# Column 0 centred only and scaled after its products; coarser weight loads; row gathers issued after the last transposes

## Chip, cores, metric

One core of one Trainium2 chip. The metric is the device time of one execution in microseconds (us). A profile's span is some 1.8 us shorter than this time. The kernel before takes 179.18 us (median of 3 runs, 179.08 to 179.73).

## The reference

```python
xn = layernorm(x)                                   # x: 2048 x 512, bf16; mean and variance by row
A  = irfft2(rfft2(xn) * (w_r + 1j * w_i))           # spectral filter
B  = (gelu(xn @ w_gate) * (xn @ w_up)) @ w_down     # 512 -> 1792 -> 512
return x + A + B
```

## The kernel before

The rows of x are kept as 16 columns of 128 rows. TensorE does both halves: the products with w_gate and w_up (`g_ps`, `u_ps`, in 14 blocks of 128 features), and the transform as products with tables (VectorE folds `A` and `xf`, then `bp`, a copy `Bs`, then `dp`, and so on). A small list scheduler written in Python orders all operations from estimated durations when the program is built. The kernel then issues them in this order on each engine. At run time semaphores alone decide when something starts, so the scheduler's durations and dependencies change the order only.

```python
    load_x(0, 1); d_ident = load_ct("ident", "ident", "ACT"); load_x(1, 1)
    load_w(0, 2, ("SP", "ACT"))     # blocks 0-1 of both weights, 256 KB each
    ...
    load_x(2, 2); load_w(2, 4); load_w(4, 6); load_x(4, 4); load_w(6, 10); load_x(8, 4); load_w(10, 14)
    ...
    def layernorm(c0, n, due, after=(), halves=1):
        ...                         # statistics, ve = var + eps (VectorE), then rstd on GpSimd:
        r = add("POOL", 0.55, lambda: nc.gpsimd.tensor_tensor(out=rstd[:, k], in0=ve[:, k], in1=half[:, k], op=ALU.pow), ...)
        ...                         # xn = (x - mean) * rstd on VectorE, in 'halves' pieces
    ...
    FIRST = [(0, 1, 0, 4), (1, 1, 0, 4), (0, 2, 4, 2), (2, 2, 0, 2), (2, 2, 2, 2), (2, 2, 4, 2)]  # column, columns, block, blocks
    for c, n, f, nf in FIRST + [(0, 4, f, 1) for f in range(6, NFC)]:
        glu(c, n, f, nf)
    ...
    def fold(cg, t):                # four columns: two operations into A, two into xf (VectorE)
        ...
        a2 = dve(0.61, f2, (a0, a1), t, new=(xb,), use=(ab,))
        a3 = dve(0.61, f3, (a2,), t, use=(ab, xb))
        for q in range(4):          # bp: the first product needs a2 only, the second needs a3
            ...
            p = pe(0.222, mm, (a2, a3, d_rf), t + 1, new=(sb,), use=(xb,))
            PS_[cg, q] = act(0.53, ev, (p,), t - 5, use=(sb,))    # ScalarE copies bp into Bs
    ...
    # rows of the filter table TW, fetched by index on GpSimd
    d_tw.append(dma(P * n * 2, lambda ...: gather(k, s, c, a, n), [g_idx] + XN[11], 20, eng="POOL", issue=1.2))
```

## Time and profile before

| | kernel before |
|---|---|
| median, 3 runs | 179.18 us |
| span of the profiled run | 177.6 us |
| TensorE busy | 98% |
| first gate matmul | 6.89 us |
| last matmul starts | 174.70 us |

The timelines: start, busy us, engine, line, operation, out<-in.

```profile
40.96 0.68 DVE L567 TENSOR_TENSOR xf<-A 128x1024 bf16<-128x1024 bf16 x1
41.89 1.06 PE L581 MATMUL bp<-RF_t,xf 128*128 128x128 bf16 x16
...
44.69 0.68 DVE L567 TENSOR_TENSOR xf<-A 128x1024 bf16<-128x1024 bf16 x1
46.24 1.06 PE L581 MATMUL bp<-RF_t,xf 128*128 128x128 bf16 x16
```

VectorE is not the bound: 40.90 of 49 us. But its third fold ends at 41.64, and the third bp starts at 41.89. The bp's second product, 0.22 us later, is the first that needs the end of the fold. So the slack there is 0.47 us (1.09 us at the fourth), in a queue that is otherwise full.

### The profile page before, as it was taken

The page shows a single profiled execution, that of the slowest core. Times are in us where ns is not written, and L with a number is a line of the kernel's source. Part 1 is how long each engine was busy: PE and PEld are TensorE (multiplying, and loading weights), DVE is VectorE, ACT ScalarE, POOL GpSimd, SP SyncE. Part 2 cuts the span into 40 slices and gives each one's busy share as a digit, 9 for nine tenths or more (in the row PEclk, how much of TensorE's full clock was granted, in tenths as well). Part 3 has the DMA queues.
Part 4 walks back from the last instruction along what each step waited for, and adds up shares of the span by engine and source line. Part 5 has one row for each costly group of instructions (what it writes and reads, how often), then busy time and mean ns, then how long its engine had stood idle before and what let it go on. Part 6 is the DMA issues. An engine that isn't in the chain of part 4 may idle for free.

```text
span 177.6 us, 3041 instructions
## 1 busy us (share of the span) xinstructions
PE 173.4 (98%) x1100; PEld 92.9 (52%) x1100; DVE 118.1 (66%) x266; ACT 87.4 (49%) x158; POOL 18.6 (10%) x33
## 2 busy tenths in 40 slices
PE   6999999999999999999999999999999999999993
PEld 2598545545554544554555455554445444544463
DVE  1869999999537995889999885336442541632522
ACT  3162437456789737999998855453111211211100
POOL 3212138743200000000000000000000000000000
PEclk9999999999999999999999999999999999999999
DMA  5999487999297001302211121100222221322212
GB/s 144 311 355 359 86 270 84 223 296 193 52 347 255 2 0 29 93 2 59 61 48 37 37 59 37 27 0 0 84 68 66 83 89 59 92 80 69 74 45 59
DMA packets 23182, 19.24 MB, mean 108 GB/s; under 512 B 8512, under 2 KB 21824, under 8 KB 23168
## 3 DMA queue, kind: packets, MB, share of 16 engines
q1 hardware_dynamic: 22176, 17.57, 35.0%
q0 software_dynamic: 320, 1.19, 3.1%
q10 hardware_dynamic: 672, 0.30, 0.6%
q8 instruction: 8, 0.13, 0.3%
q14 instruction: 6, 0.05, 0.1%
HBM read 13.28 MB, written 2.10 MB: 87 GB/s over the span
## 4 chain that ended last, share of the span: by engine, by line
PE 91%; ACT 3%; DVE 3%; issue 1%; POOL 0%; DVEq 0%; POOLq 0%
PE u_ps L502 25%; PE g_ps L502 25%; PE warm L380 3%; ACT E L652 2%; PE yp L818 2%; PE bp L581 2%; PE gp L767 2%; PE yp__2078 L872 2%; PE yp__1994 L872 2%; PE yp__1967 L872 2%; PE yp__1936 L872 2%; PE yp__1909 L872 2%; PE yp__1820 L872 2%; PE yp__1793 L872 2%; PE yp__1762 L872 2%; PE yp__1735 L872 2%
## 5 line engine op out<-in xcount | busy, mean ns | idle before, releaser
L502 PE MATMUL g_ps<-xnT,Wg_sb 128*128 128x512 bf16 (+2 forms) x264 | 58.1, 347 | 0.0
L502 PE MATMUL u_ps<-xnT,Wu_sb 128*128 128x512 bf16 (+2 forms) x264 | 57.9, 347 | 0.0
L527 DVE TENSOR_TENSOR hT<-u_ps,ge 128x512 bf16<-128x512 f32 x56 | 38.4, 685 | 17.5 <-PE u_ps L502 14.4
L519 ACT ACTIVATE ge<-g_ps 128x512 bf16<-128x512 f32 x56 | 33.5, 598 | 30.5 <-PE g_ps L502 26.5
L502 PEld LDWEIGHTS <-Wu_sb 128*128 128x128 bf16 x264 | 24.3, 98 | 22.3 <-DMA Wu_sb<-in_B_w_up_dram 0.2
L502 PEld LDWEIGHTS <-Wg_sb 128*128 128x128 bf16 x264 | 24.3, 98 | 20.7 <-issue 0.2
L872 PEld LDWEIGHTS <-hT 128*128 128x128 bf16 x252 | 23.0, 98 | 21.9
L824 ACT CAST yf<-yp 128x512 bf16<-128x512 f32 x16 | 9.3, 586 | 37.6 <-PE yp L818 37.6
L652 ACT CAST E<-ep 64x512 bf16<-64x512 f32 x32 | 18.5, 579 | 1.1 <-PE ep L646 0.7
L396 DVE BATCH_NORM_STATS2 st<-x_t 128x6 f32<-128x512 bf16 x16 | 10.5, 676 | 4.8 <-DMA x_t<-in_A_x_dram 4.8
L629 ACT CAST ds<-dp 128x512 bf16<-128x512 f32 x16 | 8.8, 589 | 1.1 <-PE dp L624 1.0
L773 ACT CAST Gs<-gp 128x512 bf16<-128x512 f32 x16 | 8.6, 593 | 1.0 <-PE gp L767 1.0
L406 POOL TENSOR_TENSOR rstd<-ve,half 128x2 f32<-128x2 f32 (+2 forms) x7 | 6.6, 949 | 21.9 <-DVE ve L404 21.9
L585 ACT CAST Bs<-bp 128x512 bf16<-128x512 f32 x16 | 8.3, 603 | 0.5 <-PE bp L581 0.5
L818 PEld LDWEIGHTS <-Gs 128*128 128x128 bf16 x64 | 4.8, 98 | 3.5
L380 PE MATMUL warm<-warm 128*128 128x512 bf16 (+1 forms) x14 | 5.1, 539 | 1.3 <-POOL half L373 1.3
L412 DVE TENSOR_SCALAR xn<-x_t,mv,rstd 128x512 bf16<-128x512 bf16 (+1 forms) x17 | 6.1, 399 | 0.3 <-POOL rstd L406 0.3
L818 PE MATMUL yp<-CT,Gs 128*128 128x128 bf16 x64 | 6.0, 219 | 0.0
L683 DVE TENSOR_TENSOR m<-X,TW 128x1024 bf16<-128x1024 bf16 x8 | 5.5, 692 | 0.2
L624 PEld LDWEIGHTS <-Bs 128*128 128x128 bf16 x64 | 4.4, 98 | 2.4
L689 DVE TENSOR_TENSOR m<-X,TW 128x1024 bf16<-128x1024 bf16 x8 | 5.5, 684 | 0.0
L646 PE MATMUL ep<-ds,CT 128*128 128x512 bf16 x16 | 5.4, 379 | 0.0
(103 smaller groups left out, 169.0 us busy)
## 6 DMA issues: line engine op xcount, KB each, us to landing
y<-in_A_x_dram SPq DMA_DIRECT2D x16, 128.0 KB, 2.1
F<-F SPq DMA_DIRECT2D x32, 64.0 KB, 2.0
out_dram<-y SPq DMA_DIRECT2D x15, 128.0 KB, 1.7
Wd_sb<-in_B_w_down_dram SPq DMA_DIRECT2D x2, 896.0 KB, 8.3
x_t<-in_A_x_dram SPq DMA_DIRECT2D x3, 512.0 KB, 6.8
Wg_sb<-in_B_w_gate_dram SPq DMA_DIRECT2D x2, 512.0 KB, 6.8
Wu_sb<-in_B_w_up_dram SPq DMA_DIRECT2D x2, 512.0 KB, 9.1
Wg_sb<-in_B_w_gate_dram SPq DMA_DIRECT2D x3, 256.0 KB, 5.1
```

The lines of the kernel that those rows point to most:

```text
L380: nc.tensor.matmul(tiles["warm"][:, 0:w], lhsT=warm[:, 0:P], rhs=warm[:, 0:w], start=True, stop=True)
L396: V.bn_stats(out=st[:], in_=x_t[:, c])
L502: nc.tensor.matmul(tiles[f"{nm}.{key}"][:, f * w:f * w + w], lhsT=W[:, e, (f0 + f) * P:(f0 + f + 1) * P], rhs=rhs(e), start=(f + e == 0), ...
L519: nc.scalar.activation(out=e[:, 0:nf * w], in_=tiles[f"g_ps.{key}"][:, 0:nf * w], func=AF.Gelu_apprx_tanh)
L527: V.tensor_tensor(out=out, in0=tiles[f"u_ps.{key}"][:, 0:nf * w].rearrange("p (f w) -> p f w", w=w) if nf > 1 else tiles[f"u_ps.{key}"][:, ...
L585: nc.scalar.copy(out=o, in_=tiles[f"bp.{cg}.{q}"][:].rearrange("p c (r g a) -> p (c r) g a", r=2, a=4))
L629: nc.scalar.copy(out=ds[:].rearrange("p (s k t) -> p s k t", s=2, t=2), in_=tiles[f"dp.{G}"][:].rearrange("p s t k -> p s k t"))
L652: nc.scalar.copy(out=tiles[f"E.{g}"][64 * h:64 * h + 64, r], in_=tiles[f"ep.{g}.{h}"][64 * r:64 * r + 64])
L773: nc.scalar.copy(out=o, in_=tiles[f"gp.{g}.{h}"][:].rearrange("p q (n a) -> p (q n) a", a=4))
L818: nc.tensor.matmul(yp[:, q], lhsT=tiles["G"][:, q, c], rhs=IQ[q], start=(q == 0), stop=(q == 3), skip_group_check=True)
L824: nc.scalar.copy(out=tiles[f"yf.{c // 2}"][:, c % 2], in_=tiles[f"yp.{c}"][:])
L872: nc.tensor.matmul(y[:, s], lhsT=tiles[sb, f][:, cl * P:(cl + 1) * P], rhs=Wd_sb[:, f, s], start=(f == 0), stop=False)
```

## The change

Intent: get TensorE to useful work earlier. Column 0 is only centred, and goes to TensorE without waiting for rstd on GpSimd. Its two PSUM tiles are scaled afterwards with 1/std, which one FP32 matmul of ones with a diagonal spreads over the partitions. The weights of the first blocks come in coarser pieces, the order of the first blocks changes, and ScalarE takes over the statistics of column 3. The planner's dependency of the gathers moves to the transposes of columns 12 to 15.

```diff
-    load_w(0, 2, ("SP", "ACT"))
+    d_g = [load_first(e, eng) for e, eng in ((0, "ACT"), (2, "SP"))]      # Wg blocks 0-3, two halves of 256 KB
+    d_u = load(..., Wu_sb[:, :, 0:4 * P] ..., land=7.0)                   # Wu blocks 0-3, 512 KB
-    load_w(2, 4)
-    load_w(4, 6)
+    load_w(4, 8, (9.2, 10.6))                                             # Wg, Wu blocks 4-7, 512 KB each
     load_x(4, 4, 12.4)
-    load_w(6, 10)
+    load_w(8, 11, (13.4, 14.4))
...
-    NWARM, NGAP, GAP = 10, 1, 4
+    NWARM, GAP = 7, 2
...
+    def column0():      # statistics; xm = x - mean in two halves; rstd and the normal xn later
+    def xm_transpose(c, os): ...
+    def spread(c):      # dg = ident * rstd; r = ones.T @ dg (FP32 matmul); Rb = copy of r
+    def layernorm_act(c, due, halves, after=(), after2=()):   # sums on ScalarE, for column 3
...
+    def glu_first(c, f0, nf):
+        ...
+            V.tensor_tensor(out=sc(k), in0=flat(("g_ps", "u_ps")[k]), in1=R(), op=ALU.mult)   # twice, VectorE
...
-    FIRST = [(0, 1, 0, 4), (1, 1, 0, 4), (0, 2, 4, 2), (2, 2, 0, 2), (2, 2, 2, 2), (2, 2, 4, 2)]
+    glu_first(0, 0, 4)
+    FIRST = [(1, 1, 0, 4), (0, 2, 4, 2), (2, 1, 0, 4), (3, 1, 0, 4), (0, 2, 6, 2), (2, 2, 4, 2), (2, 2, 6, 2)]
...
-                            [g_idx] + XN[11], 20, eng="POOL", issue=1.2))
+                            [g_idx] + [o for t in range(12, NC) for o in XT[t]], 20, eng="POOL", issue=1.2))
```

Cut: separate PSUM tiles for the two halves of a transpose, Wd in three loads instead of two, tiles that share space, and planner rules (given landing times, no hop between operations of one engine).

## The prediction

> **What bounds the kernel now.** I read the page's busy line first, then the slices, the waits of TensorE, the chain that ended last, and then the first 13 us of the timeline, because that is where the diff works.
>
> ```profile
> PE 173.4 (98%) x1100; PEld 92.9 (52%) x1100; DVE 118.1 (66%) x266; ACT 87.4 (49%) x158; POOL 18.6 (10%) x33
> PE   6999999999999999999999999999999999999993
> PE 91%; ACT 3%; DVE 3%; issue 1%; POOL 0%; DVEq 0%; POOLq 0%
> PE warm L380 <- POOL half L373: 1.3, 1, 1.3
> ```
>
> TensorE is busy for 98% of 177.6 us, carries 91% of the chain, and its only listed wait is 1.3 us ahead of the warm-up. From the first gate matmul to the last result it never visibly starves. Nothing done to VectorE, ScalarE or DMA later on can give time back; only two things can: an earlier first useful matmul, or less TensorE work after it. So the start is read instruction by instruction:
>
> ```profile
> 1.34 4.45 PE L380 MATMUL warm<-warm 128*128 128x512 bf16 x10 [1.34 <-POOL half L373]
> 3.51 0.69 DVE L396 BATCH_NORM_STATS2 st<-x_t 128x6 f32<-128x512 bf16 x1 [3.51 <-DMA x_t<-in_A_x_dram]
> 4.45 0.15 DVE L404 TENSOR_SCALAR ve<-mv 128x1 f32<-128x1 f32 x1
> 4.76 0.58 POOL L406 TENSOR_TENSOR rstd<-ve,half 128x1 f32<-128x1 f32 x1 [2.70 <-DVE ve L404]
> 5.38 0.60 DVE L412 TENSOR_SCALAR xn<-x_t,mv,rstd 128x256 bf16<-128x256 bf16 x2
> 5.78 0.65 PE L428 MATMUL tp<-CT,xn 128*128 128x128 bf16 x4
> 6.47 0.37 ACT L431 COPY xnT<-tp 128x256 bf16<-128x256 bf16 x1 [3.29 <-PE tp L428]
> 6.88 0.29 DVE L431 COPY xnT<-tp 128x256 bf16<-128x256 bf16 x1 [0.83 <-ACT xnT L431]
> 6.89 0.82 PE L502 MATMUL g_ps<-xnT,Wg_sb 128*128 128x128 bf16 x8
> 7.55 0.61 PE L502 MATMUL u_ps<-xnT,Wu_sb 128*128 128x128 bf16 x8
> 8.84 0.45 PEld L502 LDWEIGHTS <-Wu_sb 128*128 128x128 bf16 x8 [0.18 <-DMA Wu_sb<-in_B_w_up_dram]
> 11.53 1.04 PE L502 MATMUL g_ps<-xnT,Wg_sb 128*128 128x256 bf16 x8
> ```
>
> First useful matmul: 6.89. From there to 11.53 lie 64 matmuls of 128 columns and 12 transposes. Eight u matmuls from 7.55 to 8.00 give 0.056 us each, so these 76 cost 4.23 us; 4.64 us passed, 0.41 us of it lost (the wait for the second copy, a slow clock before about 7.1, 0.18 us for Wu).
>
> The second part of the change moves the row gathers, so I looked at the tile of the filter:
>
> ```profile
> L683 DVE TENSOR_TENSOR m<-X,TW x8: 682/694/696, 55.6 to 103.3; 128x1024 bf16<-128x1024 bf16 x8
> L364 POOL DMA_INDIRECT TW<-in_A_w_r_dram,idx_t x3: 947/1232/1717, 27.4 to 30.9; - x3
> L364 POOL DMA_INDIRECT TW<-in_A_w_i_dram,idx_t x3: 947/947/949, 32.2 to 34.7; - x3
> 39.51 5.16 SPq L437 DMA_TRANSPOSE xnT<-xn  x4
> 44.21 1.28 POOL L613 TENSOR_SCALAR TW<-tt 128x8 bf16<-128x8 f32 x4
> ```
>
> The gathers run at 27.4 to 35.6, the table is fixed at 45.5, and the first product that needs it starts at 55.6: 10 us of slack.
>
> **What the Trainium skill says.** "TensorE: Matmul & The Clock Gate", Part 1: at 128 columns a matmul takes 107 ns cold and 56 ns warm, and the window that decides is free-running, about 3.4 us, so the switch does not follow a count of matmuls. The trace agrees: ten warm-ups of 512 columns took 4.45 us (0.44 each), later ones of 512 columns 0.216 apart, and the 0.056 above. "PSUM — Partial Sum Buffer", PSUM bank collisions: two engines may not use the same bank and quadrant together. Agrees: the VectorE copy sat 0.83 us until ScalarE's copy from the same tile ended. "FP8 and Floating Point Precision", TensorE Precision Notes: true FP32 takes 4 passes; the kernel before has no such matmul, so no run shows it yet. "DMA: Bandwidth & Descriptors", SWDGE vs HWDGE vs iDMA: gathers built by GpSimd and the hardware queues are served round robin; the gathers landed 4.7 to 4.9 us after issue here, among other transfers.
>
> **The change part by part.**
> *Column 0 without its scale.* ve, pow and their hops go from the way: centring can start at 4.45 instead of 5.38, 0.93 us earlier. The rest of the way (transposes, copy, matmul) took 6.89 - 5.38 = 1.51 us and keeps its length: first gate matmul at 5.96. Both weight halves must be there: the 256 KB pieces issued first landed 4.2 (ScalarE queue, issued 1.12: 5.3) to 5.1 us later (issued 1.65: 6.75); the second half is wanted about 6.4 to 6.8. No clear wait.
> *What TensorE must do more after its first gate matmul.* Column 0 is transposed twice: its four normal transposes now come later, 4 x 0.056 = 0.22. One FP32 matmul of 128 columns spreads the scale: 4 x 0.056 = 0.22 (estimate from the FP8 page's four passes), with latency 0.25. Column splitting: 64 more matmuls of 128 columns for 16 fewer of 512: 64 x 0.0556 - 16 x 0.216 = 0.10. Sum 0.57.
> *Order and new waits.* The compiled order on TensorE is: 16 gate matmuls of column 0, spread, 4 transposes of column 0, 4 of column 1, then the 16 up matmuls. On VectorE, from 4.45: two centrings (0.26 apart), ve, statistics of column 1 (5.04), aggregate (5.76), copy (5.9), ve of column 1 (6.10), xn of column 0 (6.17), the diagonal (6.5). Column 1's scale: 6.10 + 0.3 + 0.62 = 7.03, its halves at 7.03 and 7.29, transposes 0.4 later: 7.43 and 7.69. So the up matmuls start at 7.8 with a fast clock. If the clock turns at 7.1 as before, the gate matmuls take 5.96 to 7.4, spread and transposes to 8.1. I take 7.95. Wu (512 KB) is wanted then; by the bytes of the first us (about 1.34 MB ahead and including it, moved by 6.8 us, plus 1 us) it lands at 7.6 to 7.9.
> Then 16 up, 32 of column 1: 48 x 0.056 = 2.67, so 10.6; plus eight transposes still to do, 0.45: 11.07 against 11.53. Gain 0.46; minus the 0.10 of the splitting, 0.36.
> *Weights of blocks 4 to 7* are now 512 KB pieces: up to Wu 2.65 MB must come in, which the bytes of before reach at 10.7, plus a landing of 1 us: 11.7, wanted at 11.5. Loss 0 to 0.3; I take 0.15.
> *ScalarE statistics of column 3, scaling of two PSUM tiles on VectorE*: ScalarE idled 1.58 and 1.33 us and VectorE 1.26 us in this stretch, so they are beside TensorE.
> *Gathers.* They wait for the last four transposes: in before issued until 44.7 and landing 3.4 later, here some 1.7 us later because one product more lies ahead: about 50. Six at 1.25 us, landing 4.8 after the last: 61.5; fix chain 2.2: 63.7. The new order puts the first product behind the first hT of the third row block, at about 65 (64.3 in before). So hidden, with 1.3 us left, and a further 1.7 us (one hT) before TensorE would starve.
> Sum: -0.36 + 0.15 = -0.2, and the tail (4.5 us from the last block's end to the last store) is unchanged. 179.18 - 0.25 = 178.9 us.
>
> **The rivals.**
> 1. *The start is won whole*: 0.93 us shows at the end because the other losses (0.41) vanish too. For it: the copies no longer share a PSUM tile. Against it: 0.57 us of added TensorE work is certain. At best 0.93 + 0.41 - 0.57 = 0.77: 178.4.
> 2. *Cold clock or column 1 takes the place of the removed wait*. Three 512-column warm-ups fewer and a gap of 0.3 us before the transposes may let the clock turn later than 7.1; each us later costs half a us: 179.4 to 179.9.
> 3. *Late table*: if gathers, now beside the 1.8 MB of Wd, land 3 us later, VectorE blocks in order, then the up tiles, then TensorE: +1 to +2: 180 to 181. For it: served round robin with hardware queues. Against it: the slack above.
> 4. *ScalarE around the first dp*: it is 97% busy from 52 to 60 already, and 16 dp now come in a row; a few waits of 0.1 to 0.3: 179.2.
>
> **Range and chances.** The best case is 178.4, losses of rivals 2 and 4 reach 179.8. Range 178.2 to 179.8. 2% is 3.6 us, over four times the largest gain at the start: faster 0.02, slower 0.03 (only rival 3 with a long stall), within 2% 0.95.
>
> **What would show it.** Right: first gate matmul near 6.0; up matmuls of column 0 near 7.9, the wait ahead of them named column 1's xn or Wu; spread about 0.3 us; first gather near 50, the table ready before 65 with no VectorE wait on GpSimd; TensorE without gaps later. Wrong: TensorE waits on m, hT or dp after 40 us; first gate matmul later than 6.3; or a summed matmul time much different from before.

## More of the kernel before

The busy time of each engine from 3 to 52 us (columns: stretch, its length, busy us with instruction counts of PE, PEld, DVE, ACT, POOL, then clock, DMA share, GB/s):

```profile
3.00:52.00 49.00, 48.95 (x364) 29.56 (x363) 40.90 (x95) 24.96 (x47) 17.06 (x25) 1.00 0.87 232
```

## The result

| | before | changed |
|---|---|---|
| median of 6 runs, one chip | 179.39 us (179.08 to 180.01) | 180.02 us (179.75 to 180.35) |
| ratio | | 1.0032, 95% interval 1.001 to 1.0055 |
| span of the profiled run | 177.6 us | 178.6 us |
| last matmul starts | 174.70 us | 175.65 us |

A ratio here is the mean time of one kernel's runs over that of the other's runs of the same rounds, so not quite the ratio of the medians. Executions over 1.5% slower than the fastest of the same kernel are left out of the means. Within 2% the kernel is as fast as before, as was most likely by the prediction. But it is 0.6 us slower where 0.25 us faster was predicted, and outside the range of 178.2 to 179.8.

The page of the changed kernel (busy time of each engine, then the engines' shares of the chain that ended last):

```profile
PE 172.3 (97%) x1136; PEld 95.0 (53%) x1153; DVE 121.3 (68%) x271; ACT 89.5 (50%) x164; POOL 17.1 (10%) x35
...
PE 65%; DVE 20%; DMA 5%; issue 4%; POOL 2%; SPq 1%; ACT 1%; DVEq 0%
```

TensorE fell from 91% of the chain to 65%. A fifth now runs over VectorE and 5% over a DMA. The waits of TensorE (what waited <- for what: us, times, longest) name both:

```profile
PE g_ps L631 <- DMA Wg_sb<-in_B_w_gate_dram: 0.5, 1, 0.5
PE u_ps L631 <- DMA Wu_sb<-in_B_w_up_dram: 0.4, 1, 0.4
PE bp L711 <- DVE xf L697: 0.2, 1, 0.2
```

The start, from the timeline of TensorE (a wait in brackets):

```profile
5.50 1.18 PE L579 MATMUL g_ps<-scr_w,Wg_sb 128*128 128x128 bf16 x16
6.57 0.46 PE L508 MATMUL r<-scr_r 128*128 128x128 f32 x2
...
7.58 1.07 PE L579 MATMUL u_ps<-scr_w,Wu_sb 128*128 128x128 bf16 x16
...
10.90 1.05 PE L631 MATMUL g_ps<-xnT,Wg_sb 128*128 128x256 bf16 x8 [0.47 <-DMA Wg_sb<-in_B_w_gate_dram]
12.38 1.05 PE L631 MATMUL u_ps<-xnT,Wu_sb 128*128 128x256 bf16 x8 [0.44 <-DMA Wu_sb<-in_B_w_up_dram]
```

The first gate matmul is 1.39 us earlier than before, earlier than predicted. Then come two stops for the weights of blocks 4 to 7. By the starts of neighbouring matmuls they cost 0.63 and 0.60 us; the listed waits are shorter because they begin at the modelled end of the matmul before. The chain within the first 16 us shows the transfer behind the second stop (start, us, what):

```profile
3.67 8.66 DMA Wu_sb<-in_B_w_up_dram
```

It was issued at 3.67 and counted as landed 8.66 us later. VectorE from 3 to 52 us, as shown of before:

```profile
3.00:52.00 49.00, 47.61 (x403) 30.93 (x406) 44.00 (x100) 25.05 (x49) 14.08 (x20) 1.00 0.79 209
```

VectorE does 3.1 us more than before in this stretch. Its third fold and the bp that needs it:

```profile
45.76 0.69 DVE L697 TENSOR_TENSOR xf<-A 128x1024 bf16<-128x1024 bf16 x1
...
45.90 0.39 PE L711 MATMUL bp<-RF_t,xf 128*128 128x128 bf16 x4
46.50 0.84 PE L711 MATMUL bp<-RF_t,xf 128*128 128x128 bf16 x12 [0.22 <-DVE xf L697]
```

By the pace of its matmuls, TensorE would have needed the fold at 46.12. The fold ends at 46.45 and TensorE goes on at 46.50: 0.33 us late, where the kernel before had 0.47 us of slack. The gathers start at 41.8 instead of 27.4, and the table they fill is used at 65.8, with no wait of VectorE for it:

```profile
L376 POOL DMA_INDIRECT TW<-in_A_w_r_dram,idx_t x3: 945/953/1104, 41.8 to 44.5; - x3
L815 DVE TENSOR_TENSOR m<-X,TW x8: 682/694/695, 65.8 to 106.2; 128x1024 bf16<-128x1024 bf16 x8
```

**A ledger that holds for all runs below.** TensorE's matmuls follow each other every 0.056, 0.109 or 0.216 us (128, 256, 512 columns). What a gap between two starts has beyond this I call a stall. From the first 512-column gate matmul of the changed kernel to the last matmul lie 152.45 us of pitches. So the start of the last matmul = arrival (start of that first 512-column matmul) + 152.45 + stalls after it. This closes to 0.03 us in every profile of a version of the changed kernel. For the kernel before, whose order differs, "arrival" is the point that leaves the same 152.45 us.

| profile | arrival | stalls after | last matmul |
|---|---|---|---|
| before | 21.96 | 0.29 | 174.70 |
| changed | 22.52 | 0.66 | 175.65 |

So 0.56 us are lost before 22 us and 0.37 us after, at the third bp. 0.28 us of stall lies near 75 to 80 us in both kernels.

These are single profiles, but those of the runs below spread little. With the front of the changed kernel (changed, e6, e10, e15) the arrival is 22.26 to 23.02. With small pieces (e1, e8, e11, e12, e18, e19) it is 21.22 to 21.45, and with the front of the kernel before (before, e9, e13, e14), counted as in the table, 21.83 to 21.96.

### The profile page after: what moved, and what is told of

Read it like the earlier page. It is cut to its first block, busy times and chain, and to the rows that moved or that the text cites. A ratio compares the mean times of both kernels' runs of the same rounds, so it can differ in the third digit from the quotient of the medians.

```text
span 178.6 us, 3142 instructions
## 1 busy us (share of the span) xinstructions
PE 172.3 (97%) x1136; PEld 95.0 (53%) x1153; DVE 121.3 (68%) x271; ACT 89.5 (50%) x164; POOL 17.1 (10%) x35
## 4 chain that ended last, share of the span: by engine, by line
PE 65%; DVE 20%; DMA 5%; issue 4%; POOL 2%; SPq 1%; ACT 1%; DVEq 0%
PE u_ps L631 15%; PE g_ps L631 13%; DVE hT L656 7%; DMA Wu_sb<-in_B_w_up_dram 5%; DVE st L408 3%; DVE xn L440 2%; PE yp L955 2%; PE gp L899 2%; PE yp__2148 L1009 2%; PE yp__2122 L1009 2%; PE yp__2006 L1009 2%; PE yp__1979 L1009 2%; PE yp__1832 L1009 2%; PE yp__1776 L1009 2%; PE yp__2064 L1009 2%
## 5 line engine op out<-in xcount | busy, mean ns | idle before, releaser
L631 PE MATMUL u_ps<-xnT,Wu_sb 128*128 128x512 bf16 (+2 forms) x267 | 56.0, 338 | 0.8 <-DMA Wu_sb<-in_B_w_up_dram 0.4
L631 PE MATMUL g_ps<-xnT,Wg_sb 128*128 128x512 bf16 (+2 forms) x265 | 55.4, 337 | 0.7 <-DMA Wg_sb<-in_B_w_gate_dram 0.5
L656 DVE TENSOR_TENSOR hT<-u_ps,ge 128x512 bf16<-128x512 f32 x55 | 37.5, 684 | 16.7 <-PE u_ps L631 14.3
L648 ACT ACTIVATE ge<-g_ps 128x512 bf16<-128x512 f32 x55 | 32.9, 599 | 28.9 <-PE g_ps L631 28.2
L434 POOL TENSOR_TENSOR rstd<-ve,half 128x1 f32<-128x1 f32 (+2 forms) x7 | 6.3, 899 | 29.7 <-DVE ve L416 29.2
L899 PEld LDWEIGHTS <-F 128*128 128x128 bf16 x64 | 4.4, 98 | 2.4 <-issue 0.2
L899 PE MATMUL gp<-CT,F 128*128 128x128 bf16 x64 | 5.2, 219 | 0.1
```

The source lines that it names most:

```text
L631: nc.tensor.matmul(tiles[f"{nm}.{key}"][:, f * w:f * w + w], lhsT=W[:, e, (f0 + f) * P:(f0 + f + 1) * P], rhs=rhs(e), start=(f + e == 0), ...
L648: nc.scalar.activation(out=e[:, 0:nf * w], in_=tiles[f"g_ps.{key}"][:, 0:nf * w], func=AF.Gelu_apprx_tanh)
L656: V.tensor_tensor(out=out, in0=tiles[f"u_ps.{key}"][:, 0:nf * w].rearrange("p (f w) -> p f w", w=w) if nf > 1 else tiles[f"u_ps.{key}"][:, ...
L899: nc.tensor.matmul(gp[:, q], lhsT=F[:, h, q % 2, q // 2::2], rhs=cc("M" if 2 * g + h else "M0"), start=(q == 0), stop=(q == 3), skip_group ...
```

## The experiments

The theory at first, L: the weight waits are the whole loss. Rivals that came up: V, VectorE is full up to the folds, so that a gain at the front ends in a wait for `xf`. And H, the gathers on GpSimd delay TensorE's semaphore increments, so that the engines that wait for it start late. The 18 runs were on three chips: the first eight on one (called a), e10 to e13, e18 and e19 on b, e14 to e17 on c. Every ratio is to the kernel before on the same chip. The kernel before is not equally quiet everywhere: on chip a eight of its twelve runs took 179.2 to 179.8 us and four 181.1 to 181.8. This makes many intervals wide, so I read the ledger first.

### e1_small: blocks 4 to 7 in pieces of 256 KB

```diff
-    load_w(4, 8, (9.2, 10.6))
+    load_w(4, 6, (8.8, 9.5))
+    load_w(6, 8, (10.1, 10.6))
```

> The changed kernel, but the gate and up weights of blocks 4 to 7 come in four 256 KB transfers (blocks 4-5 of both, then 6-7 of both) instead of two of 512 KB; TensorE's order is untouched. Theory L (the coarse pieces make TensorE wait): the waits of 0.63 and 0.60 us ahead of the first blocks 4-5 matmuls (at 10.90 and 12.38) shrink to under 0.2 together, and the time falls by about 1.0 us, from 180.0 to 179.0 (0.997 to 0.998 of the kernel before). Rival A (added TensorE work and column splitting are the loss, the bytes in all are the same): waits and time stay, 179.8 to 180.2.

180.31 us (180.02 to 180.53), ratio 0.9998 (0.994 to 1.005). Arrival at 21.32: 1.2 us earlier, both weight waits gone. But 1.48 us of stalls follow. The waits of TensorE, and one line of ScalarE's timeline:

```profile
PE bp L712 <- ACT Bs L718: 0.6, 1, 0.6
...
49.42 0.59 ACT L718 CAST Bs<-bp 128x512 bf16<-128x512 f32 x1 [1.55 <-PE bp L712]
```

ScalarE sat idle for 1.55 us waiting for a bp product that TensorE had done by 46.2, some 3 us before. The matmuls had run and the news came late. Read with the Trainium skill, "Perfetto Trace Analysis", Tensor Engine Instruction: a matmul's end in a profile is estimated, and its semaphore update follows only when PSUM has acknowledged the write. The trace agrees that there is a delay. That it can be microseconds is what this run adds. L alone falls.

### e2_late and e3_small_late: TensorE held back on purpose

```diff
 def warm_mm(w):
     if "warm" not in tiles:
+        for _ in range(3):                      # three more warm-ups of 512 columns at the start
+            nc.tensor.matmul(tiles["warm"][:, 0:w], lhsT=warm[:, 0:P], rhs=warm[:, 0:w], start=True, stop=True)
```

> The changed kernel with three more warm-up matmuls of 512 columns ahead of column 0, in the same order otherwise: a pure delay of the first gate matmul by about 1.2 us (5.5 to 6.7). Theory L: the weights of blocks 4 to 7 land when they land, so the delay is taken out of the two waits, and the time rises by at most 0.3 us (180.0 to 180.3). Rival S (the start sets the end): the time rises by the whole delay, to 181.2.

e2 (the changed kernel so delayed): 180.63 us (179.95 to 181.07), ratio 1.0021. Its first gate matmul is at 6.47, 1 us later. It arrives at 21.82 without weight waits, 0.7 us earlier than the changed kernel. That is not theory L as written, by which the weights land when they land: the up matmuls of block 4 started at 11.68 with no listed wait, so Wu was there by then and not at 12.34. Why it landed sooner, no run shows.

> Both edits together: small pieces and the pure delay of 1.2 us. Theory L: with the small pieces the wait no longer hides the delay, so this run is slower than the small pieces alone by 0.8 to 1.2 us: about 180.0, the time of the changed kernel. Rival A: delay costs the same with and without the small pieces.

e3 (small pieces as well): 180.81 us (180.18 to 181.03), ratio 1.0022. Arrival 21.80, stalls 1.47 us, again at bp for Bs. Its first gate matmul is 1.1 us later than that of e1, its arrival only 0.48 us and its median 0.50 us later, under the 0.8 to 1.2 us expected. So even with small pieces the start alone does not set the arrival; e16 comes back to this. The times are too noisy on this chip to say more.

### e4_big: blocks 4 to 10 in one piece of 896 KB for each weight

```diff
-  q.dma_start(out=t[:, :, a:b], in_=v[:, :, a:b])
+  end = 11 * P if f0 == 4 else b               # one load covers blocks 4-10; the load of 8-10 is dropped
+  None if f0 == 8 else q.dma_start(out=t[:, :, a:end], in_=v[:, :, a:end])
```

> The suspected cost doubled: blocks 4 to 10 of each weight in one 896 KB transfer, nothing else moved. By the bytes (393 KB more ahead of gate, 786 KB more ahead of up, at about 0.36 MB per us) theory L expects gate to land at 12.0 and up at 14.6, the waits to grow from 1.2 to about 3.4 us, and the time by 2.0 to 2.3 us: 182.1. Rival A: no change, 180.0.

183.29 us (182.25 to 187.05; the highest is a slow run, and the median of the other five is 182.78), ratio 1.016 (1.009 to 1.023). From TensorE's timeline:

```profile
11.64 1.05 PE L632 MATMUL g_ps<-xnT,Wg_sb 128*128 128x256 bf16 x8 [1.51 <-DMA Wg_sb<-in_B_w_gate_dram]
...
13.98 0.28 PE L632 MATMUL u_ps<-xnT,Wu_sb 128*128 128x256 bf16 x1 [1.29 <-DMA Wu_sb<-in_B_w_up_dram]
```

By the starts these are 1.68 and 1.46 us, together 1.9 us more than in the changed kernel. Arrival is 1.6 us later than in the changed kernel and the last matmul 1.9 us later (177.57). So more bytes in the pieces mean a later landing, and a longer wait is paid in full. But taking the wait away (e1) was not paid back in full: something else takes over.

### e5_undo: without the trick of column 0

```diff
-    o_xm = column0()
-    xm_transpose(0, o_xm); spread(0); pe_transpose(0, 10.4)
+    layernorm(0, 1, -80, (), 2)
+    pe_transpose(0, -40)
-    glu_first(0, 0, 4)
-    FIRST = [(1, 1, 0, 4), ...]
+    FIRST = [(0, 1, 0, 4), (1, 1, 0, 4), ...]
```

Column 0 is handled like column 1; the planner orders the rest anew.

> The changed kernel without the trick of column 0: it is normalised and transposed like column 1, the spread matmul, its copy, the two scalings and the second transposes of column 0 are gone; loads, order of blocks, gathers and the statistics of column 3 stay. If the trick is worth what the timeline says (first gate matmul 5.50 against 6.89, less 0.52 us of added TensorE work), the first gate matmul falls back to about 6.8 and column 1 is done some 0.5 us later than in the changed kernel, but the weight waits of blocks 4 to 7 take up the difference: they shrink by the same 0.5 us, so the time stays at 179.9 to 180.1. Rival (the trick is worth its 0.5 us at the end): 180.4 to 180.6.

180.46 us (180.20 to 180.70), ratio 1.0012. The first gate matmul is at 6.29, 0.8 us later than in the changed kernel, and no weight wait is listed. Arrival is 22.34, within the changed kernel's own spread, so with 512 KB pieces no gain of the trick shows by 22 us. But this profile does not show why. Its matmuls kept the slow pace, 0.107 us from start to start, until 8.86: from the first gate matmul to the first of column 1 it took 3.26 us, where e16 took 2.01 us for the same instructions. So it came late for the weights by the clock and did not wait for them.

### e6_pure: the gathers back before the last rstd, nothing else moved

```diff
     order = plan.run()
+    gathers = [o for o in d_tw if o.eng == "POOL"]
+    pool = [o for o in order if o.eng == "POOL"]
+    last_pow = pool[pool.index(gathers[0]) - 1]
+    order = [o for o in order if o not in gathers]
+    k = order.index(last_pow)
+    order[k:k] = gathers
```

> The changed kernel with one thing undone: the six row gathers stand again ahead of the last rstd in GpSimd's queue (they start at about 28 us instead of 41.8); every other instruction of every engine keeps its place. Theory H (the late gathers, beside the DMA transposes of columns 12 to 15, hold up the filter's front): the waits of TensorE at bp and dp around 40 to 55 us (0.2 to 0.4 us in the changed kernel's profile) vanish, the two weight waits (0.5 and 0.4 us) stay; 179.6 to 179.8 us, ratio to the kernel before about 1.001. Rival X (those waits come from VectorE's fold, which the new order of blocks puts later): the wait of bp for xf stays at 0.2 and the time at 180.0.

180.69 us (180.50 to 180.78), ratio 1.002. It is not faster. The third bp now waits 0.6 us for xf instead of 0.2. In the trace, TensorE's increments from 32.7 to 36.5 us come about 0.75 us apart, also those of a bp group, which come 0.22 us apart in the changed kernel. The gathers run until 36.0. VectorE idles 0.42 us there for TensorE. So the form of H that I wrote down, "late gathers are the fault", is wrong: early ones hurt too, by another way.

### e8_small_gather: small pieces and early gathers

Both edits together (e1 and e6).

> Small weight pieces for blocks 4 to 7 (as in the run with small pieces) and the gathers ahead of the last rstd. Theory H: with neither weight waits nor late gathers the one microsecond won at the front is kept: no wait of bp for ScalarE's Bs, first full gate matmul near 21.5 us, span 177.0 to 177.3, time 178.8 to 179.1, ratio 0.997. Rival X: TensorE still waits 0.5 to 1 us at bp for Bs and xf, since it arrives there earlier than ScalarE and VectorE; time 179.6 to 180.0.

180.18 us (179.82 to 180.86), ratio 0.9995. Arrival 21.40, stalls 1.36, of which 0.7 are the third bp's wait for xf. A miss, above both ranges that were expected: the stall is the one at the fold, as the rival said.

### e9_before_late: the kernel before with late gathers

The reverse of e6: in the kernel before the six gathers move behind the last rstd.

> The kernel before with one thing changed: its six gathers stand behind the last rstd in GpSimd's queue, so they start near 39.5 instead of 27.4 us; nothing else moves. Theory H: waits of 0.5 to 1 us appear ahead of bp or dp between 44 and 54 us, time 179.9 to 180.3, ratio 1.003 to 1.006. Rival X: the table is late but still ready by about 51, before the first product at 55.6; no new wait; 179.2 to 179.4, ratio 1.000.

180.50 us (180.08 to 180.71), ratio 1.0014 (0.994 to 1.009). The profile shows a wait that the kernel before did not have, where H puts it:

```profile
PE dp L624 <- ACT Bs L585: 0.3, 1, 0.3
```

Stalls by 52 us are 0.67 us. The time lies 1.0 us above the median of the eight usual runs of the kernel before on this chip (179.54), but by the ratio, over all its runs, no difference is shown.

### e13_before: the kernel before once more, as a control

No edit.

> The kernel before itself under another name, as a control: ratio 1.000, and the half width of its interval is what a difference must exceed. Its runs here should fall into the same two groups as those of the kernel before on this chip (179.2 to 179.8, and some at 181.1 to 181.8). If its profile falls into the second group it shows where the 1.6 us lie: theory H says in a burst of late increments during its gathers at 27 to 36 us.

180.14 us (179.53 to 180.72), ratio 0.9997 (0.995 to 1.004). The interval's half width, 0.45%, is what a difference must exceed on this chip. The runs did not fall into the two groups that were expected. Its profile caught what the first profile of the same program had not. VectorE's timeline and TensorE's waits:

```profile
37.25 0.69 DVE L527 TENSOR_TENSOR hT<-u_ps,ge 128x512 bf16<-128x512 f32 x1 [0.76 <-PE u_ps L502]
...
PE bp L581 <- DVE xf L567: 0.8, 1, 0.8
```

In the first profile that hT ran at 36.48 with no wait. Here VectorE waited 0.76 us for a product that was done, its folds came 1.2 us later, and the third bp waited 0.8 us. So neither effect is new: the kernel before has them in some of its executions.

The delivery times of TensorE's increments, read from the trace records of each run (times agree with the timeline to about 0.3 us):

```
run    gathers on GpSimd   gap before      then a burst of increments ~0.06 us apart
e1     40.7 to 48.0 us     2.14 us         7 from 49.64
e2     41.1 to 48.5 us     0.76 us         7 from 50.10
e3     41.1 to 48.5 us     1.44 us         7 from 50.11
e4     43.4 to 50.8 us     0.75 us         7 from 52.42
e5     40.0 to 48.1 us     1.45 us         4 from 49.21
e8     26.8 to 35.0 us     1.00 us         4 from 36.25
e9     38.8 to 46.7 us     1.44 us         7 from 48.14
e12    26.8 to 35.0 us     0.93 us         4 from 36.18
e13    27.3 to 35.5 us     1.70 us         5 from 37.23
e15    42.3 to 49.7 us     1.46 us         7 from 51.38
e16    39.7 to 47.5 us     1.67 us         5 from 48.85
e17    29.7 to 37.9 us     3.07 us         4 from 39.58
no burst of four or more: before, changed, e6 (slowed, see above), e10, e11, e18, e19; and e14, which has no gathers
```

Where the gathers moved, the hold moved with them, and each burst came 1 to 2 us after the last gather. The gap just before the burst need not be the longest: in e3 and e15 an earlier one was 3.1 us. And four of the profiles without a burst are not free of it: e10, e11, e18 and e19 each have two increments 0.06 us apart within or just after their gathers (50.43 and 50.49 in e11), and by the same records some increments come up to about 1.1 us after the modelled end of their matmuls. No stall came of it.

### e14_plain: the kernel before without gathers

```diff
-        nc.gpsimd.indirect_dma_start(out=TW[:, k, s, a:a + n], out_offset=None, in_=w_in[:, :], in_offset=...)
+        nc.sync.dma_start(out=TW[:, k, s, a:a + n], in_=w_in[0:1024].rearrange("(p g) k -> p (g k)", g=8)[:, 0:n])
```

Plain loads of the same size from SP, of other rows: the result is wrong (relative error 0.030).

> The kernel before with its six gathers replaced by plain loads of other rows, of the same size and place in the plan, issued by SP; GpSimd gathers nothing. The result is wrong on purpose (wrong filter rows). The control run of the kernel before had TensorE increments held back from 35.5 to 37.2 us and then 0.8 us of waiting at the third bp for VectorE. Theory H (the gathers on GpSimd hold the increments back): no burst of late increments, no wait at bp, all runs in 179.3 to 179.8. Rival (something else holds them back, and the gathers only happen to lie there): the burst, the bp wait and runs above 180 stay.

179.45 us (179.19 to 179.66), while the kernel before took 180.29 (179.80 to 181.55) on this chip: ratio 0.9947 (0.992 to 0.998). The third bp, which had waited in the control:

```profile
41.76 1.06 PE L579 MATMUL bp<-RF_t,xf 128*128 128x128 bf16 x16
```

Sixteen in one piece, no wait; no burst; and no run above 179.7. Taking the gathers off GpSimd takes away the holds and the high runs at once. This run also changed how six transfers are made, so it shows that the gathers are the source and not which part of them. The six times carry more weight here than the one profile, as the first profile of the kernel before had no hold either.

### e17_before_dose: the kernel before with more VectorE work early

```diff
         V.bn_stats(out=st[:], in_=x_t[:, c])
+        if c in (4, 5, 6):
+            V.bn_stats(out=st[:], in_=x_t[:, c])
```

> The kernel before with three statistics of VectorE done twice (columns 4, 5, 6), some 1.9 us more of VectorE work at 12 to 16 us; nothing else. Theory V (from 12 to 46 us VectorE is full, so what is added early arrives late at the folds, where TensorE waits): a wait of about 1.2 to 1.8 us for xf at the third or fourth bp, time up by 1 to 1.6 us: 180.7 to 181.3. The prediction's view (work of VectorE early lies beside TensorE): 179.4 to 179.8.

182.04 us (181.62 to 184.46; the highest is a slow run), ratio 1.0083 (1.005 to 1.012). By the medians 1.75 us more, for some 1.9 us of VectorE work, placed right behind the spot where, by the prediction's own reading, VectorE idles for 1.26 us. TensorE's waits:

```profile
PE u_ps L504 <- DVE hT L529: 1.7, 2, 1.4
...
PE bp L583 <- DVE xf L569: 0.5, 1, 0.5
```

The size is as V says, but the place was a surprise: most of it stops TensorE at once, because a full u_ps ring waits for VectorE's hT. The rest comes at the fold, where this profile also has a hold. VectorE work at 12 to 16 us is not "beside TensorE" in the kernel before. The run does not test the work that the change itself adds, most of it before 11 us.

### e10_fold: the third fold ahead of the normalisation of columns 12 to 15

```diff
     order = plan.run()
+    late = [o for c in (12, 13, 14) for o in XN[c]]
+    moved = [o for c in (12, 13, 14) for o in XT[c]]
+    ...      # h1, h2: the two hT that follow in VectorE's queue
+    order[k:k] = fold3[:2]              # A and xf of the third fold right behind h1
+    order[k:k] = fold3[2:] + late + moved   # the second xf behind h2, then xn 12-14 and their DMA transposes
```

> The changed kernel with one thing moved: in VectorE's queue the last three operations of the third fold (A, and both xf) stand ahead of the normalisation of columns 12 to 15 instead of behind it, some 1.5 us earlier; the DMA transposes of 12 to 14 move with their columns. Every other engine keeps its order. Theory V (VectorE is full from 16 to 50 us, partly with work the change gave it, and TensorE meets its last folds with no slack): the wait of the third bp for xf (0.2 us listed) vanishes, the fold ends near 43.6 instead of 46.4; the two weight waits stay, so 179.8 to 180.0 us, span about 0.2 us less than the changed kernel's. Rival (the wait is from late semaphores, not from the order): the wait stays.

179.68 us (179.25 to 180.02), ratio 0.9976 (0.993 to 1.002). From the timelines of VectorE and TensorE:

```profile
42.94 0.68 DVE L697 TENSOR_TENSOR xf<-A 128x1024 bf16<-128x1024 bf16 x1
...
45.63 1.06 PE L711 MATMUL bp<-RF_t,xf 128*128 128x128 bf16 x16
```

The fold ends 2 us before it is wanted, and not 0.3 us after. Arrival 22.26, stalls 0.28, which is all that the kernel before has too. The effect is read from the ledger: the times alone do not show it, and 0.26 us of the gain against the changed kernel's profile lie in the arrival.

### e11_small_fold: small pieces and the earlier fold

e1 and e10 together, with the gathers where the change put them.

> Small weight pieces for blocks 4 to 7, the third fold earlier in VectorE's queue as in the run before, gathers where the change put them (late). Theory V alone: no weight waits, no bp wait for xf: 179.0 to 179.2. Theory V with H (the late gathers hold back TensorE's semaphore increments between 45 and 50 us, so that ScalarE copies Bs late): a wait of 0.5 to 1 us at the fourth bp or at dp stays, its increments arrive in one burst near 49 to 50 us; 179.7 to 180.1.

179.25 us (178.95 to 179.41) beside 179.79 (179.44 to 181.54) of the kernel before: ratio 0.9951 (0.991 to 0.999). Arrival 21.45, stalls 0.27, last matmul 174.16, the first version that keeps what the front wins.

### e12_small_fold_gather: the same with early gathers

The edits of e1, e10 and e6 together.

> Small weight pieces, third fold earlier, gathers early (about 27 to 35 us). If V and H are both right, nothing makes TensorE wait between 7 and 75 us for more than 0.2 us: the 0.5 to 1 us of the front arrive at the end; span 177.0 to 177.4, time 178.8 to 179.2, faster than the kernel before by 0.2 to 0.4 per cent. If increments held back at 29 to 36 us still make VectorE wait (0.4 to 0.7 us in the two runs with early gathers), the folds end that much later but have now 1.5 us of slack, so the time still holds. Rival: 179.6 or more, with a wait that moved elsewhere.

180.82 us (179.95 to 181.55), ratio 1.0043. A miss, and the opposite of what I expected. The second bp now waits:

```profile
36.44 0.84 PE L712 MATMUL bp<-RF_t,xf 128*128 128x128 bf16 x12 [0.78 <-DVE xf L698]
```

The hold from early gathers falls upon the second fold, which has no slack, as only the third had been moved. With the third fold early, the late place that the change gave the gathers is the better one of the two.

### e15_after: the changed kernel again

No edit.

> The changed kernel itself, on the same chip as these others, so that the versions without its waits can be compared with it. 179.9 to 180.4, ratio to the kernel before between 1.000 and 1.004; its profile shows the two weight waits, the wait of the third bp for xf, and perhaps late increments between 45 and 50 us.

180.57 us (180.34 to 181.68), more than expected, beside 180.29 of the kernel before, ratio 1.0015 (0.998 to 1.005). The profile is of the slowest of these runs: arrival 23.02, stalls 1.51.

```profile
PE bp L711 <- ACT Bs L717: 0.7, 1, 0.7
```

The changed kernel itself also has executions with the hold, then at the fourth bp.

### e16_small_fold_undo: small pieces and the earlier fold, without the trick

The edits of e1, e5 and e10 together.

> Small weight pieces and the third fold earlier, as in the fastest version so far (179.25), but without the trick of column 0. What the trick is worth once nothing behind it gives it back: the timeline says the first gate matmul comes 0.9 to 1.3 us later without it, and 0.52 us of TensorE work are saved (spread 0.30, four transposes 0.22), so it should be slower by 0.4 to 0.8 us: 179.6 to 180.0. If the trick is worth nothing even then: 179.2.

182.61 us (181.49 to 183.03), ratio 1.011. Far slower than expected, but not for the trick: the planner orders this version anew, and its fourth bp waits for xf (with a hold in this profile):

```profile
PE bp L709 <- DVE xf L695: 1.6, 1, 1.6
```

The time therefore says nothing about the trick. The arrival, 22.07 against 21.45 (e11) and 21.22 (e19), does not either: 0.63 us of it are a stop of TensorE for VectorE's hT at 17.1 us, which e11 and e19 do not have:

```profile
PE u_ps L630 <- DVE hT L655: 0.5, 1, 0.5
```

What the trick is worth is seen before that stop, from the timelines of TensorE, first e16 and then e11:

```profile
6.64 1.05 PE L630 MATMUL g_ps<-xnT,Wg_sb 128*128 128x128 bf16 x16
7.75 1.06 PE L630 MATMUL u_ps<-xnT,Wu_sb 128*128 128x128 bf16 x16
10.43 1.04 PE L630 MATMUL g_ps<-xnT,Wg_sb 128*128 128x256 bf16 x8
...
5.46 0.61 PE L580 MATMUL g_ps<-scr_w,Wg_sb 128*128 128x128 bf16 x8
7.75 1.07 PE L580 MATMUL u_ps<-scr_w,Wu_sb 128*128 128x128 bf16 x16
10.44 1.04 PE L632 MATMUL g_ps<-xnT,Wg_sb 128*128 128x256 bf16 x8
```

The trick starts the gate matmuls 1.2 us earlier, and the up matmuls of column 0 start at the same time. Between them lie the spread, the second transposes and gaps in which TensorE waits. Block 4 is reached at 10.43 without the trick and at 10.21 to 10.44 in the six profiles with it and with small pieces. So the trick is worth 0 to 0.2 us there. This is one profile without it, from a run whose time was a miss.

### e18_four and e19_again: the fastest version, with four gathers and with six

e19 is e11 once more. e18 fetches the unmirrored first rows with plain loads:

```diff
-        nc.sync.dma_start(out=TW[64 * h:64 * h + 64, k, 0, KC:], in_=rows[0, h][:, :, KC:8 * KC])
+        nc.sync.dma_start(out=TW[64 * h:64 * h + 64, k, 0, :], in_=rows[0, h])
+        if h == 0:                                                # eight special rows
+            nc.sync.dma_start(out=TW[32:64:4, k, 0, 0:KC], in_=w.rearrange("(i r) k -> r i k", r=P)[64, 0:8])
```

> The fastest version so far (small weight pieces, third fold earlier) with four gathers on GpSimd instead of six: the unmirrored first rows come with the plain loads of their neighbours, and one small plain load puts the eight special rows in. Right result. Theory H: GpSimd is done with gathers some 2.5 us earlier, so fewer increments can be held back in the stretch of the third and fourth bp and of dp: no slower than the version with six, 178.9 to 179.4, runs close together. Rival: the gathers do not matter once the folds have slack: the same time to 0.1.

> The fastest version so far (small weight pieces, third fold earlier, six late gathers) on this chip beside the version with four gathers: 179.0 to 179.5, ratio to the kernel before 0.994 to 0.998, with fewer high runs than the kernel before. If its profile catches late increments at 45 to 51 us, it also shows whether its slack covers them: no wait at bp above 0.3 us.

e18: 179.10 us (178.78 to 179.31), ratio 0.9937 (0.991 to 0.997). e19: 179.10 us (178.79 to 179.56), ratio 0.9943 (0.991 to 0.998), beside 180.14 (179.51 to 181.51) of the kernel before. Arrivals 21.45 and 21.22, stalls 0.39 and 0.29, no burst of four or more. Four gathers or six make no difference here. Both beat the kernel before by 0.6% on the same chip. The changed kernel was not run on this chip; with the kernel before as the yardstick it stands at 1.0015 to 1.0032, so they beat it too.

## Why the prediction was wrong

Point by point, by its own steps.

**First gate matmul and up matmuls of column 0: the numbers too cautious, the reason not borne out.** Predicted 5.96 and 7.95, measured 5.50 and 7.58. That made the front 0.37 us better than planned. But the prediction puts its gain down to the scale that goes from the way, and e16 without the trick has the up matmuls at 7.75 and reaches block 4 as early as the versions with it. That the front is ahead of the kernel before (block 4 wanted at 10.27, against 11.53 less 0.45 for eight transposes) is, by that one profile, in the main due to the rest of the change. Rival 1's reason fits: in e16 the 64 matmuls and 4 transposes up to block 4 take 3.79 us, 0.056 each, so the losses of 0.41 us are gone. Which edit removed them, no run shows. Of rival 2, the half about column 1 is what happened, without making the front late. Its half about the clock was small here. In e1's profile the 16 first gate matmuls were busy for 1.68 us instead of 1.18, their starts 0.107 us apart up to about 6.7, and the up matmuls began at 7.64 instead of 7.58; in e6, slow up to about 7.1, at 7.82. But e5 lost 1.2 us to the slow pace. One reading was off without harm: the first 256 KB piece on SP is put at 6.75 by the page's median of 5.1 us, and its own landing is at 5.85. And one agreement claims too much: the 0.83 us that VectorE's copy stood still is a wait at a semaphore, which the program sets, so it does not show the rule of the PSUM page.

**More work on TensorE: right.** Predicted 0.57 (its parts add up to 0.54), measured about 0.62 us (spread 0.30, transposes 0.22, splitting 0.10).

**Weights of blocks 4 to 7: the term that was mis-sized.** "Loss 0 to 0.3; I take 0.15" measured 1.23 us. The landing of Wu ends the loss; the stop for Wg before it is a part of the same. Two figures were off. The time of need (11.5) came from a front that still had eight transposes ahead of it; they were put later, so the up matmuls were wanted at 11.14 (eight pitches of 0.109 after 10.27). And Wu landed at 12.34, not 11.7. With the 0.2 us between 11.5 and 11.7 that makes 0.2 + 0.36 + 0.64 = 1.20. e1 removes the stops, e4 makes them larger by the expected kind of step. The landing also differs between executions: Wu was there by 11.68 in e2, and TensorE went on at 12.87 in e15.

**"So they are beside TensorE": the step whose mechanism failed.** I saw idle VectorE time near 12 us and let the added work (two scalings, centring, a diagonal) vanish into it. By 52 us VectorE does 3.1 us more, and from 16 to 50 us it is busy for 32.98 of 34 us, against 30.43 before. In the changed order the third fold ends 0.33 us after TensorE wants it. This costs 0.37 us by the ledger. What is worse, it caps the front: any gain upstream of it turns into a wait there, as e1 (0.45 us at the third bp) and e8 show. e10 gives the fold 2 us and the wait goes; e17 shows from the other side that early VectorE work is paid by TensorE. What is not separated is why the fold is late: e10 moves the order and not the work, so the added work and the planner's new order, which puts the fold behind the normalisation of columns 12 to 15, can both have a part.

**Gathers "hidden": right about the table, wrong about the start, blind to the rest.** The prediction has them wait for the last transposes and start at about 50. That dependency is the planner's alone; on the chip they started at 41.81, right behind the last rstd (done at 41.63). The table was ready about 53.3 and used at 65.8, with no wait. Rival 3 looked at the same place and for the wrong thing. What the gathers do is hold TensorE's increments back, in a burst in 12 of the 19 profiles that have them. Where they were moved, so was the hold. The first comparison did not catch this, its two profiles have no burst. It widens both kernels' runs.

**Rival 4 (ScalarE around the first dp)** was never the cause: where ScalarE was late, it was waiting for news from TensorE.

**The sum.** Predicted -0.21 at the end. Minus 0.37 (start, the longer spread included), plus 1.08 (weights), plus 0.37 (third bp): +0.87 us; the last matmul of the two profiles differs by +0.95. The medians differ by 0.63. The profiled run of the changed kernel is one of its two slowest.

**What stays open.** Which part of a gather holds the increments back, and why some executions have no hold. e10, e11, e18 and e19, all with late gathers and the earlier third fold, had no burst of four or more in four profiles; whether the order prevents it or chance does is not shown. And about 0.3 us of the fastest version are lost after its last matmul (span minus last matmul 3.2 to 3.3 us instead of 2.9), which no run was spent on.

## What to carry to other kernels

When a stage is sped up, ask what the same engine waits for next and how much slack that has, before counting the gain: here the first gate matmul came 1.4 us earlier, but its own added work and the wait for column 1 took most of that, and what the rest of the change won at the front was lost first to 512 KB pieces and then to a fold that ended too late. To learn what one edit of several is worth, look for the first place where all versions do the same work, as block 4 in e16. An engine with idle time at one place is not free, if its queue is full from there to the next place where the bound engine needs it. When an engine waits for a product that the timeline shows as done, look at when the semaphore increment was delivered, and at what GpSimd gathers at that time.

## What the Trainium skill lacked or had wrong

- No page has that gathers on GpSimd can hold back TensorE's semaphore increments; "DMA: Bandwidth & Descriptors", SWDGE vs HWDGE vs iDMA, would be the place. Holds of 0.75 to 3.1 us in 12 of 19 profiles, and 180.29 against 179.45 us for the kernel before with and without gathers.
- "Perfetto Trace Analysis", Tensor Engine Instruction, says that a matmul's update follows after its estimated end, without a size: up to 3 us were seen (e1: products done by 46.2, ScalarE started at 49.42).
- "FP8 and Floating Point Precision", TensorE Precision Notes, has four passes for true FP32: the 128-column spread showed as two matmul records and took 0.28 to 0.30 us on TensorE, against 0.22 that four passes of 0.056 would give.
- "TensorE: Matmul & The Clock Gate", Part 1, gives the turn to the full rate a run-to-run spread of 500 ns either way. In five profiles with the same warm-up from 1.34 us on (changed, e1, e4, e6, e8) it came between about 4.8 us (e4) and 7.1 us (e6), 3.5 to 5.8 us after the first matmul.
